# Attention followed by an ELU feed-forward layer on one core: block products in slots of seven, and q and k of batches 3 to 7 turned by DMA through DRAM

## The chip, the core and the metric

The kernel runs on one of the eight cores of a Trainium2 chip. A core has TensorE (PE in the profile; PEld is its weight load), VectorE (DVE), ScalarE (ACT), GpSimd (POOL) and SyncE (SP), each with its own instruction queue that runs in program order; they meet at semaphores. DMA transfers are issued from SP's, ACT's or POOL's queue and are carried by 16 DMA engines. The metric is the device time of one execution in microseconds; each figure below is the median of several runs.

## The reference, cut to what matters

```python
# q, k, v: [B=8, H=8, S=576, D=64]; beacon_k, beacon_v: [8, 8, 16, 64]
k_all = concat([beacon_k, k], axis=2)          # 592 keys
v_all = concat([beacon_v, v], axis=2)
scores = (q @ k_all.T) / sqrt(D)               # causal among the 576, all 16 beacons seen
a = softmax(scores)
attn = a @ v_all                               # [8, 8, 576, 64]
x = attn as [4608 tokens, 512]
h = x @ w_in                                   # w_in [512, 2048]
g = where(h > 0, h, exp(min(h, 0)) - 1)        # ELU
out = g @ w_out                                # w_out [2048, 512], out [4608, 512] fp32
```

## The kernel before

**Attention.** It works batch by batch, and within a batch by pairs of heads `p` = 0 to 3 (two heads of 64 fill 128 partitions). The scores are computed with keys on the partitions and queries along the free dimension, so q and k are both needed with D on the partitions ("turned"). `load_qk` (L117) casts q and k from fp32 to bf16 while loading them into stage tiles `qst` and `kst` (two buffers each) of 96 partitions, six consecutive rows of the sequence on each partition, in runs of 384 numbers. `T` (L225) turns a pair with 24 small PE transposes (12 of q, 12 of k) into a PSUM tile of the tag `S`; `ck` (L248) copies that tile with ACT into one of four `qk` tiles, putting the rows back in order; `cb` (L242) puts the beacon keys into the first 16 columns with DVE.

`S` (L266) computes a quarter of a pair's scores into a PSUM tile of the tag `S` (two buffers), `x` (L286) takes their exponential with ACT, `m` (L292) masks the diagonal blocks with DVE. `L` and `W` (L323, L361) multiply the exponentials with ones and with v for four heads at a time; their results lie in tiles of the tag `S` too. `n` (L342) turns the sums into reciprocals with ACT (logarithm, then exponential, tile `rl`), and `M` (L390) multiplies by them with DVE and so writes `xT`, the input of the feed-forward layer. `R` (L412) does the last 64 queries of a batch in the same way. `load_v` (L124) loads v with GpSimd, the beacon values first and then five transfers, into one of two buffers.

**Feed-forward layer.** The tokens are cut into ten tiles `t` (two of 256, eight of 512). `F` (L427) computes 128 of the 2048 columns of `h` with four matmuls of 512 columns into one of two PSUM banks `hps`; `e` (L444), `r` (L449) and `g` (L455) make the ELU of it with ACT, DVE and DVE, and `g` writes it to `gt`. From tile 2 on, the second product is a block scheme with seven products instead of eight: the sums of blocks that it needs are made by `wt` (L506, of the weights) and `Z` (L506 to L516, of `gt`) with DVE; each of the seven phases of `PH` (L519) is 16 matmuls of 256 columns, eight for each half `qd`, accumulated in two PSUM tiles. `J` (L536) takes a phase's result away: phases 0, 2 and 3 by an ACT copy to `sm`, phases 1, 4 and 5 by a DVE addition to `osb`, phase 6 by an ACT copy to `osb`; SP's queue stores each `osb` (three buffers).

**Order.** The order on every engine is the order in which the program is written. Up to the end of tile 2 it is written out by hand, as a list of words such as `S.2.0.1` (L573 to L607). From then on a loop over `b` = 3 to 10 writes it (L628): for each of 16 slots `i`, first the ELU column `F e r g` of tile `b`, then, in the 14 slots of `HS`, one half phase `Q` of tile `b-1` and, after its second half, `J`; then the sums `Z` that `SUMS` puts there; then what `todo` holds for the slot of batch `b`: scores (`SC`), `L` and `W` (`LW`, `WR`), and up to `b` = 7 the transposes `T_` of the last pair of batch `b` and of three pairs of batch `b+1`. At `i` = 3 the loads of batch `b+1` are issued on POOL, q and k (`lk`) and then v (`lv`).

Of the kernel before, what the change touches and what calls it, by code (L numbers as in the profile page):

```python
# [10 lines left out]
BF16 = mybir.dt.bfloat16  # L11
# [6 lines left out]
def kernel(  # L18
# [21 lines left out]
    R = 6  # L40
# [4 lines left out]
    NKC = (SK + P - 1) // P  # L45
# [24 lines left out]
    NFC = DF // P  # L70
# [6 lines left out]
    _sets = list(get_activation_tables(nc.m.arch).items())  # L77
    _set_id = next(i for i, (nm, fs) in enumerate(_sets) if _needed.issubset(fs))

    konst = ctx.enter_context(tc.tile_pool(name="konst", bufs=1))  # L80
    stage = ctx.enter_context(tc.tile_pool(name="stage", bufs=2))
    attn = ctx.enter_context(tc.tile_pool(name="attn", bufs=2))
    xpool = ctx.enter_context(tc.tile_pool(name="xpool", bufs=3))
# [8 lines left out]
            name=nc.get_next_instruction_name(),  # L92
# [9 lines left out]
    NPR = NFC // 2  # L102
# [9 lines left out]
    def new_stage(b):  # L112
        qst = stage.tile([PR, H, R, D], BF16, tag="qst")
        kst = stage.tile([PR, H, R, D], BF16, tag="kst")
        st.setdefault(b, [None] * 3)[0:2] = [qst, kst]

    def load_qk(b, h0, h1):  # L117
        for src, dst in ((q, st[b][0]), (k, st[b][1])):
            nc.gpsimd.dma_start(
                out=dst[:, h0:h1, :, :].rearrange("p h r d -> p h (r d)"),  # L120
                in_=src[b, h0:h1, :, :].rearrange("h (p r) d -> p h (r d)", r=R),
            )
# [39 lines left out]
    for t in qks:  # L162
# [4 lines left out]
    bkT = konst.tile([P, NP, P], BF16)  # L167
# [7 lines left out]
        out=triu, in_=triu, compare_op=ALU.is_ge, fill=0.0, base=0,  # L175
# [13 lines left out]
    op = {}  # L189
# [31 lines left out]
    tps, qkT, sc, ets = {}, {}, {}, {}  # L221
# [98 lines left out]
    lt, ut, rls = {}, {}, {}  # L320
# [185 lines left out]
    def Z(t, n, h_):  # L506
# [8 lines left out]
        else:  # L515
# [3 lines left out]
    PH = [(0, (0, 0), B11, True), (1, (1, 0), B21, True), (0, (0, 0), T2, False), (1, (0, 1), T1, True),  # L519
          (0, None, B12, False), (1, (1, 0), B22, False), (0, (1, 1), T4, False)]  # L520

    @step
    def Q(t, ph, qd):

        if (t, 0) not in xy:
            for n_ in (0, 1) if t % 2 == 0 else (1, 0):
                xy[t, n_] = psum.tile([P, 2, HM], FP32, tag="ops", name="ops")
        n_, src, wt_, first = PH[ph]
        for c in range(NPR):
            lw = s3[:, c] if src is None else A(t, c // HP, *src)[:, c % HP]  # L530
            nc.tensor.matmul(  # L531
                out=xy[t, n_][:, qd, :], lhsT=lw[:, P * qd:P * (qd + 1)], rhs=wt_[:, c, :],
                start=(first and qd == 0 and c == 0), stop=(c == NPR - 1), skip_group_check=True)
# [20 lines left out]
    def wo(i):  # L554
        load_wo(i)

    @step
    def lk(b):
        new_stage(b)
        load_qk(b, 0, H)  # L560

    @step
    def lv(b):
# [24 lines left out]
    F.1.0 r.1.1 g.1.1 S.1.3.2 e.1.0 m.1.3.0 r.1.0 x.1.3.2 S.1.2.0 x.1.2.0 F.1.2 G.0.0.1 g.1.0 e.1.2  # L588
    S.1.3.3 S.1.2.1 m.1.3.2 F.1.5 m.1.2.0 x.1.3.3 cb.2.2 x.1.2.1 r.1.2 S.1.2.2 e.1.5 g.1.2 F.1.3
    m.1.3.3 G.0.1.1 x.1.2.2 m.1.2.1 r.1.5 e.1.3 g.1.5 m.1.2.2 S.1.2.3 r.1.3 T.2.0 x.1.2.3 ck.2.0  # L590
    g.1.3 F.1.6 F.1.7 S.2.0.0 S.2.0.1 e.1.6 cb.3.0 x.2.0.0 x.2.0.1 G.0.0.2 S.2.0.2 m.1.2.3 x.2.0.2
    G.0.1.2 T.2.1 r.1.6 g.1.6 e.1.7 m.2.0.0 T.2.2 m.2.0.1 ck.2.1 m.2.0.2 G.0.0.3 ck.2.2 L.1.0 r.1.7
    W.1.0.0 g.1.7 S.2.0.3 o.0.0 n.1.0 cb.2.3 F.1.4 M.1.0.0 x.2.0.3 e.1.4 m.2.0.3 G.0.1.3 r.1.4
    W.1.0.1 o.0.1 L.1.1 M.1.0.1 g.1.4 W.1.1.0 n.1.1 W.1.1.1 M.1.1.0 R.1 S.2.1.0 M.1.1.1 x.2.1.0
    G.1.1.0 n.1.R m.2.1.0 M.1.R F.2.1 F.2.0 e.2.1 S.2.1.1 S.2.1.2 e.2.0 r.2.1 g.2.1 G.1.1.1 r.2.0
    F.2.2 x.2.1.1 S.2.2.0 x.2.1.2 S.2.2.1 g.2.0 m.2.1.1 e.2.2 F.2.3 x.2.2.0 m.2.1.2 x.2.2.1 r.2.2
    G.1.0.0 e.2.3 g.2.2 m.2.2.0 m.2.2.1 r.2.3 F.2.4 S.2.2.2 g.2.3 e.2.4 S.2.1.3 cb.3.2 x.2.2.2 r.2.4
    g.2.4 G.1.1.2 F.2.5 m.2.2.2 T.3.0 x.2.1.3 m.2.1.3 e.2.5 T.2.3 ck.3.0 ck.2.3 F.2.6 r.2.5 G.1.1.3
    g.2.5 e.2.6 S.2.2.3 S.2.3.0 F.2.8 o.1.1 cb.3.1 x.2.2.3 G.1.0.1 r.2.6 x.2.3.0 S.2.3.1 m.2.2.3
# [24 lines left out]
    SLOTS = [0, 1, 2, 4, 5, 6, 7, 8, 9, 11, 12, 13]
    HS = [0, 1, 2, 3, 4, 5, 7, 8, 9, 10, 11, 12, 14, 15]
    SUMS = {0: [(-1, 1, 1)], 2: [(-1, 2, 0)], 3: [(-1, 2, 1)], 5: [(-1, 4, 0)], 7: [(-1, 4, 1)],
            11: [(0, 3, 0)], 13: [(0, 1, 0)], 15: [(0, 3, 1)]}
    for b in range(3, NT // TT + 2):  # L628
        todo = {}
        if b < B:  # L630
            todo = dict(zip(SLOTS, [
                lambda: SC(b, 1, 0), lambda: SC(b, 1, 2), lambda: (T_(b, 3), LW(b, 0)),
                lambda: SC(b, 2, 0), lambda: SC(b, 2, 2), lambda: (T_(b + 1, 0), WR(b, 0)),
                lambda: SC(b, 3, 0), lambda: SC(b, 3, 2), lambda: (T_(b + 1, 1), LW(b, 1)),
                lambda: SC(b + 1, 0, 0), lambda: SC(b + 1, 0, 2), lambda: (T_(b + 1, 2), WR(b, 1))]))
# [18 lines left out]
_INS = ['q', 'k', 'v', 'beacon_k', 'beacon_v', 'moe_w_in', 'moe_w_out']  # L654
_OUTS = [((4608, 512), 'float32')]
# [25 lines left out]
```

## Time and profile before

| | us |
|---|---|
| median of the 3 runs shown | 377.95 |
| lowest and highest of them | 377.32 and 377.96 |
| the profiled execution, its own time | 377.59 |
| its span, from the first to the last instruction | 375.9 |

| engine | busy, us | share of the span |
|---|---|---|
| PE, matmul | 352.2 | 94% |
| DVE | 286.5 | 76% |
| ACT | 253.7 | 67% |
| PE, weight load | 219.8 | 58% |
| POOL | 68.5 | 18% |

The granted TensorE clock was 0.997 over the span. The software DMA queue (POOL's) carried 54,720 packets and 18.49 MB, SP's queue 9,856 packets and 9.57 MB. HBM read was 37.22 MB, written 9.44 MB.

How to read the rows that follow. A group of instructions: line, engine, operation, output <- input by the program's names (`sc` scores, `et` exponentials, `tp` transposed pair, `hps` columns of h, `ops` block products), shapes, xcount | busy us, mean ns of one | idle time of the engine just before them, and what ended most of it. A row of a timeline: start in us, us, engine, line, operation, and in brackets the idle time before it with what ended it. A row of windows: the stretch, its length, then busy us and instruction count of PE, PEld, DVE, ACT and POOL, the granted clock, the share of the 16 DMA engines (can exceed 1, where packets overlap) and GB/s. A row of waits: who <- for whom: us in total, times, longest.

### The profile page before, as it was taken

How to read it: one execution, taken by the hardware profiler on the slowest of the kernel's cores; microseconds unless marked ns; L12 is line 12 of the kernel's file. 1: busy time of each engine (PE TensorE's matmuls, PEld its weight loads, DVE VectorE, ACT ScalarE, POOL GpSimd, SP SyncE). 2: the span in 40 equal slices, each digit the busy share in tenths (PEclk: the TensorE clock that was granted, in tenths of full speed). 3: DMA queues.
4: the chain of work that ended last, by engine and by line, in shares of the span. 5: the costliest groups of instructions: out<-in, count | busy, mean ns of one | idle time of the engine just before them, and what ended most of it. 6: DMA issues, size and time to landing. Idle time of an engine off the chain costs nothing.

```text
span 375.9 us, 11164 instructions
## 1 busy us (share of the span) xinstructions
PE 352.2 (94%) x4811; PEld 219.8 (58%) x4811; DVE 286.5 (76%) x675; ACT 253.7 (67%) x383; POOL 68.5 (18%) x100
## 2 busy tenths in 40 slices
PE   7989999999888999899989999899989998998985
PEld 3567666454555665566655666566645665665674
DVE  2448877779788697787877787868878888888861
ACT  2999996887676867697668768686767354344321
POOL 8876630410330004100510040000000000000000
PEclk9999999999999999999999999999999999999998
DMA  8999999963298019900973057001000100110112
GB/s 117 170 186 197 179 190 196 74 103 81 17 59 149 3 58 95 151 6 30 102 101 77 14 71 70 28 2 59 31 28 2 60 28 30 47 39 29 56 58 85
DMA packets 65201, 28.89 MB, mean 77 GB/s; under 512 B 41088, under 2 KB 63616, under 8 KB 65152
## 3 DMA queue, kind: packets, MB, share of 16 engines
q0 software_dynamic: 54720, 18.49, 44.7%
q1 hardware_dynamic: 9856, 9.57, 7.7%
q8 instruction: 37, 0.61, 0.7%
q10 hardware_dynamic: 576, 0.13, 0.2%
q14 instruction: 12, 0.10, 0.1%
HBM read 37.22 MB, written 9.44 MB: 124 GB/s over the span
## 4 chain that ended last, share of the span: by engine, by line
PE 57%; DVE 20%; ACT 10%; issue 5%; POOL 3%; DMA 3%; ACTq 0%; DVEq 0%; POOLq 0%
PE hps L436 22%; PE ops L531 18%; DVE gt L459 5%; PE lt L314 5%; PE sc L277 5%; ACT et L287 4%; DVE r L451 4%; PE ops L468 3%; DVE xT L384 3%; PE tp L235 3%; DVE osb L547 3%; DVE gt L489 2%; DMA kst<-in_k_dram 2%; PE ut L314 2%; ACT rl L350 2%
## 5 line engine op out<-in xcount | busy, mean ns | idle before, releaser
L436 PE MATMUL hps<-xT,w_in 128*128 128x512 f16 (+1 forms) x640 | 147.7, 359 | 4.4 <-DVE gt L459 3.5
L446 ACT ACTIVATE e<-hps 128x512 f32<-128x512 f32 x144 | 86.5, 601 | 53.4 <-PE hps L436 52.2
L287 ACT ACTIVATE et<-sc 128x832 f16<-128x832 f32 x128 | 104.2, 873 | 21.3 <-PE sc L277 21.3
L459 DVE TENSOR_TENSOR gt<-hps,r 128x512 f16<-128x512 f32 x144 | 99.6, 691 | 6.5 <-PE sc L277 0.5
L531 PEld LDWEIGHTS <-gt 128*128 128x128 f16 x768 | 74.5, 98 | 38.0 <-DVE gt L489 11.5
L436 PEld LDWEIGHTS <-w_in 128*128 128x128 f16 x640 | 56.3, 97 | 51.7 <-issue 12.0
L451 DVE TENSOR_SCALAR r<-e 128x512 f16<-128x512 f32 x144 | 62.5, 434 | 16.2 <-ACT e L446 14.4
L531 PE MATMUL ops<-wt,gt 128*128 128x256 f16 x384 | 50.5, 273 | 9.3 <-DVE gt L489 9.3
L303 DVE TENSOR_TENSOR et<-et,triu 128x256 f16<-128x256 f16 (+2 forms) x164 | 39.8, 271 | 23.3 <-ACT et L287 21.8
L531 PE MATMUL ops<-w_out,gt 128*128 128x256 f16 x384 | 49.1, 273 | 0.0
L277 PE MATMUL sc<-qk 64*128 64x208 bf16 (+9 forms) x528 | 36.6, 249 | 2.0 <-ACT et L287 1.1
L256 ACT COPY qk<-tp 128x1152 bf16<-128x1152 bf16 x29 | 32.5, 1134 | 3.9 <-PE tp L235 3.8
L132 POOL DMA_DIRECT2D v<-in_v_dram x40 | 34.2, 885 | 4.6 <-DMA kst<-in_k_dram 2.6
L489 DVE TENSOR_TENSOR gt<-gt 128x1024 f16<-128x1024 f16 x48 | 32.5, 682 | 0.1
L277 PEld LDWEIGHTS <-qk 64*128 64x128 bf16 x528 | 19.0, 94 | 22.6 <-issue 16.0
L314 PEld LDWEIGHTS <-v 128*32 128x32 f16 x1248 | 21.2, 94 | 9.2 <-issue 2.5
L127 POOL DMA_DIRECT2D v<-in_beacon_v_dram x8 | 4.3, 534 | 115.0 <-PE ut L314 115.0
L384 DVE TENSOR_TENSOR xT<-lt,rl 128x448 f16<-128x448 f32 (+6 forms) x28 | 10.6, 419 | 15.4 <-ACT rl L350 15.4
L547 DVE TENSOR_TENSOR osb<-ops,sm 128x512 f32<-128x512 f32 x24 | 16.4, 682 | 5.6 <-issue 4.6
L540 ACT COPY sm<-ops 128x512 f32<-128x512 f32 x24 | 14.1, 586 | 8.3 <-PE ops L531 8.3
L314 PE MATMUL ut<-et,v 128*32 128x64 f16 (+6 forms) x840 | 16.9, 224 | 1.1 <-issue 0.6
L468 PE MATMUL ops<-w_out,gt 128*128 128x512 f16 x64 | 16.5, 380 | 0.0
(55 smaller groups left out, 249.2 us busy)
## 6 DMA issues: line engine op xcount, KB each, us to landing
out_dram<-osb SPq DMA_DIRECT2D x36, 256.0 KB, 2.2
qst<-in_q_dram POOLq DMA_DIRECT2D x6, 576.0 KB, 6.5
kst<-in_k_dram POOLq DMA_DIRECT2D x6, 576.0 KB, 9.4
v<-in_v_dram POOLq DMA_DIRECT2D x24, 128.0 KB, 5.1
w_in<-in_moe_w_in_dram POOLq DMA_DIRECT2D x16, 128.0 KB, 5.3
w_out<-in_moe_w_out_dram POOLq DMA_DIRECT2D x4, 512.0 KB, 11.0
v<-in_v_dram POOLq DMA_DIRECT2D x8, 112.0 KB, 3.3
v<-in_v_dram POOLq DMA_DIRECT2D x8, 80.0 KB, 5.2
```

The lines of the kernel that those rows point to most:

```text
L132: nc.gpsimd.dma_start(out=st[b][2][r0:r0 + n, j, :, :], in_=v[b, :, ilo[j]:ilo[j] + n, :].rearrange("h s d -> s h d"),)
L256: nc.scalar.copy(out=t[:, :, NB:SK].rearrange("c i (p r) -> c i p r", r=R), in_=tps[b, p][:, :, 0:S].rearrange("c i (r p) -> c i p r", r=R))
L277: nc.tensor.matmul(out=s[:, h, a - c0:e - c0], lhsT=t[D * h:D * (h + 1), 1, P * j:P * (j + 1)], rhs=t[D * h:D * (h + 1), 0, NB + qa + a - ...
L287: nc.scalar.activation(out=ets[b, p][:, :, GW * g:GW * (g + 1)], in_=sc[b, p, g][:, :, 0:GW], func=AFT.Exp, bias=0.0, scale=SCALE)
L303: nc.vector.tensor_tensor(out=o, in0=o, in1=triu[0:kc[j], :, t0:t0 + e - a], op=ALU.mult)
L314: nc.tensor.matmul(out=t[32 * i:32 * (i + 1), a - qa:e - qa], lhsT=ones[0:kc[j], :] if half is None else v16[0:kc[j], j, h, 32 * half:32 * ...
L436: nc.tensor.matmul(out=h[:, n_, :], lhsT=w_in16[:, cc, P * fc:P * (fc + 1)], rhs=xt[k][:, cc, a - TT * k:e - TT * k], start=(cc == 0), sto ...
L446: nc.scalar.activation(out=eb[t, i], in_=flat(hp[t, i]), func=AFT.Exp, bias=0.0, scale=1.0)
L451: nc.vector.tensor_scalar(out=rb[t, i], in0=eb[t, i], scalar1=1.0, scalar2=1.0, op0=ALU.min, op1=ALU.subtract)
L459: nc.vector.tensor_tensor(out=gh[k][:, i % UN, :], in0=flat(hp[t, i]), in1=rb[t, i], op=ALU.max)
L489: nc.vector.tensor_tensor(out=o_, in0=a_, in1=b_, op=op_)
L531: nc.tensor.matmul(out=xy[t, n_][:, qd, :], lhsT=lw[:, P * qd:P * (qd + 1)], rhs=wt_[:, c, :], start=(first and qd == 0 and c == 0), stop= ...
```

## The change

Three things are changed.

1. **Block products.** `Q` takes a range of the 112 matmuls of a tile (7 phases x 2 halves x 8) instead of a phase and a half. Each of the 16 slots gets `NQ` = 7 of them; `HS` goes. `J` of a phase is written behind the slot in which its last matmul lies (`i` = 2, 4, 6, 9, 11, 13 and 15). In `SUMS` two sums move one slot ahead: the second half of sum 4 from `i` = 7 to 6, the first half of sum 1 from 13 to 12.
2. **q and k from batch 3 on.** `lk` casts q and k of a batch with two GpSimd DMAs from DRAM to DRAM into a bf16 scratch laid out by row [S, H, D] (two buffers each). A new step `lt` issues four DMA transposes on SP's queue, each turning 576 rows of 256 columns (two pairs) into half of a stage tile that now holds the turned q and k of two pairs; GpSimd writes the zeros behind the keys and copies the beacon keys. `T`, `ck` and `cb` of these batches go. In the loop `lt` of batch `b+1` is written at `i` = 1, `lv` of batch `b+1` stays at `i` = 3, and `lk` of batch `b+2` comes at `i` = 4. In the list `lt.3` stands where `T.3.0` stood, and `lk.4` is added near its end.
3. **Three sums of tile 2** (`Z.2.3.0`, `Z.2.1.0`, `Z.2.3.1`) move from the head of `b` = 3 into the last lines of the list.

```diff
+    BD = 3
+    dram = ctx.enter_context(tc.tile_pool(name="dram", bufs=2, space=bass.MemoryType.DRAM))
...
-    def Q(t, ph, qd):
+    def Q(t, k0, k1):
...
-        n_, src, wt_, first = PH[ph]
-        for c in range(NPR):
+        for k_ in range(k0, k1):
+            ph, qd, c = k_ // (2 * NPR), k_ // NPR % 2, k_ % NPR
+            n_, src, wt_, first = PH[ph]
...
     def lk(b):
-        new_stage(b)
-        load_qk(b, 0, H)
+        if b < BD:
+            new_stage(b)
+            load_qk(b, 0, H)
+            return
+        for n_, src in enumerate((q, k)):
+            t = scr[b, n_] = dram.tile([S, H, D], BF16, tag=f"scr{n_}", name="scr")
+            nc.gpsimd.dma_start(out=t[:, :, :], in_=src[b].rearrange("h s d -> s h d"))
+
+    @step
+    def lt_(b):
+
+        for x_, tag in enumerate(("qst", "kst")):
+            t = stage.tile([P, 2, 2, P * NKC], BF16, tag=tag, name="qkd")
+            for n_ in range(2):
+                nc.sync.dma_start_transpose(
+                    out=t[:, :, n_, NB:SK],
+                    in_=scr[b, n_].rearrange("s h d -> s (h d)")[:, 2 * P * x_:2 * P * (x_ + 1)])
+            nc.gpsimd.memset(t[:, :, 1, SK:P * NKC], 0.0)
+            nc.gpsimd.tensor_copy(out=t[:, :, 1, 0:NB], in_=bkT[:, 2 * x_:2 * x_ + 2, NB * b:NB * (b + 1)])
+            for y in range(2):
+                qkT[b, 2 * x_ + y] = t[:, y, :, :]
...
-    HS = [0, 1, 2, 3, 4, 5, 7, 8, 9, 10, 11, 12, 14, 15]
-    SUMS = {0: [(-1, 1, 1)], 2: [(-1, 2, 0)], 3: [(-1, 2, 1)], 5: [(-1, 4, 0)], 7: [(-1, 4, 1)],
-            11: [(0, 3, 0)], 13: [(0, 1, 0)], 15: [(0, 3, 1)]}
+    NQ = 14 * NPR // NFC
+    SUMS = {0: [(-1, 1, 1)], 2: [(-1, 2, 0)], 3: [(-1, 2, 1)], 5: [(-1, 4, 0)], 6: [(-1, 4, 1)],
+            11: [(0, 3, 0)], 12: [(0, 1, 0)], 15: [(0, 3, 1)]}
...
         if b == 3:
-            run("wt.3.0 wt.3.1 Z.2.3.0 Z.2.1.0 Z.2.3.1")
+            run("wt.3.0 wt.3.1")
...
-            if i in HS:
-                n_ = HS.index(i)
-                run(f"Q.{b - 1}.{n_ // 2}.{n_ % 2}")
-                if n_ % 2:
-                    run(f"J.{b - 1}.{n_ // 2}")
+            run(f"Q.{b - 1}.{NQ * i}.{NQ * (i + 1)}")
+            for ph in range(7):
+                if NQ * i < 2 * NPR * (ph + 1) <= NQ * (i + 1):
+                    run(f"J.{b - 1}.{ph}")
...
+            if i == 1 and b + 1 < B:
+                run(f"lt.{b + 1}")
+            if i == 4 and b + 2 < B:
+                run(f"lk.{b + 2}")
             if i == 3 and b + 1 < B:
-                run(f"lk.{b + 1} lv.{b + 1}")
+                run(f"lv.{b + 1}")
```

More of the change, by code (lines that the diff above doesn't have):

```diff
@@ L555, in wo @@
         load_wo(i)
+    scr, qkd = {}, {}
     @step
     def lk(b):
-        new_stage(b)
-        load_qk(b, 0, H)
+        if b < BD:
[17 more added lines that the diff above has]
+                qkT[b, 2 * x_ + y] = t[:, y, :, :]
+    op["lt"] = lt_
     @step
@@ L590 @@
     m.1.3.3 G.0.1.1 x.1.2.2 m.1.2.1 r.1.5 e.1.3 g.1.5 m.1.2.2 S.1.2.3 r.1.3 T.2.0 x.1.2.3 ck.2.0
-    g.1.3 F.1.6 F.1.7 S.2.0.0 S.2.0.1 e.1.6 cb.3.0 x.2.0.0 x.2.0.1 G.0.0.2 S.2.0.2 m.1.2.3 x.2.0.2
+    g.1.3 F.1.6 F.1.7 S.2.0.0 S.2.0.1 e.1.6 x.2.0.0 x.2.0.1 G.0.0.2 S.2.0.2 m.1.2.3 x.2.0.2
     G.0.1.2 T.2.1 r.1.6 g.1.6 e.1.7 m.2.0.0 T.2.2 m.2.0.1 ck.2.1 m.2.0.2 G.0.0.3 ck.2.2 L.1.0 r.1.7
@@ L596 @@
     F.2.2 x.2.1.1 S.2.2.0 x.2.1.2 S.2.2.1 g.2.0 m.2.1.1 e.2.2 F.2.3 x.2.2.0 m.2.1.2 x.2.2.1 r.2.2
-    G.1.0.0 e.2.3 g.2.2 m.2.2.0 m.2.2.1 r.2.3 F.2.4 S.2.2.2 g.2.3 e.2.4 S.2.1.3 cb.3.2 x.2.2.2 r.2.4
-    g.2.4 G.1.1.2 F.2.5 m.2.2.2 T.3.0 x.2.1.3 m.2.1.3 e.2.5 T.2.3 ck.3.0 ck.2.3 F.2.6 r.2.5 G.1.1.3
-    g.2.5 e.2.6 S.2.2.3 S.2.3.0 F.2.8 o.1.1 cb.3.1 x.2.2.3 G.1.0.1 r.2.6 x.2.3.0 S.2.3.1 m.2.2.3
+    G.1.0.0 e.2.3 g.2.2 m.2.2.0 m.2.2.1 r.2.3 F.2.4 S.2.2.2 g.2.3 e.2.4 S.2.1.3 x.2.2.2 r.2.4
+    g.2.4 G.1.1.2 F.2.5 m.2.2.2 lt.3 x.2.1.3 m.2.1.3 e.2.5 T.2.3 ck.2.3 F.2.6 r.2.5 G.1.1.3
+    g.2.5 e.2.6 S.2.2.3 S.2.3.0 F.2.8 o.1.1 x.2.2.3 G.1.0.1 r.2.6 x.2.3.0 S.2.3.1 m.2.2.3
     L.2.0 e.2.8 x.2.3.1 W.2.0.0 g.2.6 W.2.0.1 m.2.3.0 s.0.0 r.2.8 g.2.8 s.0.1 m.2.3.1 F.2.7 wt.1.0 n.2.0
@@ L603 @@
     F.2.10 wt.2.1 x.2.3.3 G.1.0.3 e.2.10 S.3.0.2 m.2.3.3 o.1.0 x.3.0.2 S.3.0.3 F.2.12 wt.4.0 r.2.10 m.3.0.2 g.2.10
-    L.2.1 e.2.12 W.2.1.0 x.3.0.3 s.1.0 r.2.12 F.2.14 wt.4.1 g.2.12 m.3.0.3 n.2.1 M.2.1.0 F.2.13 e.2.14
-    T.3.1 W.2.1.1 e.2.13 r.2.14 R.2 ck.3.1 T.3.2 g.2.14 r.2.13 F.2.15 g.2.13 M.2.1.1 n.2.R M.2.R
-    e.2.15 r.2.15 ck.3.2 g.2.15
-    """)
-    def T_(b, p):
-        if b < B:
-            run(f"cb.{b}.{p} T.{b}.{p} ck.{b}.{p}")
+    L.2.1 e.2.12 W.2.1.0 x.3.0.3 s.1.0 lk.4 r.2.12 F.2.14 wt.4.1 g.2.12 Z.2.3.0 m.3.0.3 n.2.1 M.2.1.0 F.2.13 e.2.14
+    W.2.1.1 e.2.13 r.2.14 R.2 g.2.14 Z.2.1.0 r.2.13 F.2.15 g.2.13 M.2.1.1 n.2.R M.2.R
+    e.2.15 r.2.15 g.2.15 Z.2.3.1
+    """)
     def SC(b, p, g0):
@@ L631 @@
             todo = dict(zip(SLOTS, [
[L632 to L635, printed above, removed]
+                lambda: SC(b, 1, 0), lambda: SC(b, 1, 2), lambda: LW(b, 0),
+                lambda: SC(b, 2, 0), lambda: SC(b, 2, 2), lambda: WR(b, 0),
+                lambda: SC(b, 3, 0), lambda: SC(b, 3, 2), lambda: LW(b, 1),
+                lambda: SC(b + 1, 0, 0), lambda: SC(b + 1, 0, 2), lambda: WR(b, 1)]))
         if b == 3:
-            run("wt.3.0 wt.3.1 Z.2.3.0 Z.2.1.0 Z.2.3.1")
+            run("wt.3.0 wt.3.1")
         for i in range(NFC):
```

## The prediction

> **What bounds the kernel now.** I read the page first, then the waits, then one stage at a time. A stage is one round of the loop over `b`, cut at the first `F` matmul of each tile; a slot is one value of its inner index `i`.
>
> ```profile
> span 375.9 us, 11164 instructions
> PE 352.2 (94%) x4811; PEld 219.8 (58%) x4811; DVE 286.5 (76%) x675; ACT 253.7 (67%) x383; POOL 68.5 (18%) x100
> ```
>
> The table of windows (us; then busy us and instructions of PE, PEld, DVE, ACT, POOL; clock; DMA share; GB/s) has `b` = 5, 7, 8 and 10:
>
> ```profile
> core 0: us, PE busy (x) PEld busy (x) DVE busy (x) ACT busy (x) POOL busy (x), PEclk, DMA share, GB/s
> ...
> 184.01:224.37 40.36, 38.94 (x576) 24.42 (x576) 32.28 (x78) 30.42 (x47) 6.33 (x9) 1.00 0.53 72
> ...
> 264.74:302.68 37.94, 36.01 (x489) 22.24 (x489) 30.69 (x70) 24.68 (x40) 0.00 (x0) 1.00 0.09 30
> 302.68:330.38 27.70, 26.53 (x176) 17.09 (x176) 24.02 (x44) 11.53 (x20) 0.00 (x0) 1.00 0.11 38
> ...
> 358.09:375.90 17.81, 12.56 (x114) 10.79 (x111) 6.84 (x11) 2.93 (x5) 0.00 (x0) 0.94 0.22 74
> ```
>
> In a full stage PE works 38.94 of 40.36 us and everything else has room: PE's own work sets the period, and DVE, at 32.28, is the next bound. Most of the 1.42 us that PE is idle has one cause, which the waits (total, times, longest) name:
>
> ```profile
> PE ops L531 <- DVE gt L489: 9.3, 8, 1.3
> ```
>
> Eight times, once for each `b` from 3 to 10, the block products wait for a sum `Z`. The timelines of PE and of DVE show why:
>
> ```profile
> 196.87 0.61 PE L531 MATMUL ops<-wt,gt 128*128 128x256 f16 x4 [1.29 <-DVE gt L489]
> ...
> 195.53 0.68 DVE L547 TENSOR_TENSOR osb<-ops,sm 128x512 f32<-128x512 f32 x1
> 196.13 0.68 DVE L489 TENSOR_TENSOR gt<-gt 128x1024 f16<-128x1024 f16 x1
> ```
>
> At `i` = 3 `J` of phase 1 is written ahead of `Z.2.1`. It cannot run before phase 1 has ended, so `Z` ends 0.7 us later still, and the fifth product of phase 2, which reads it, stands.
>
> **Part 1: PE transposes and their copies go** (20 pairs: all of batches 3 to 7). First the groups of the stage `b` = 5, then PE's order at one pair:
>
> ```profile
> L235 PE MATMUL tp<-identb,qst 96*64 96x96 bf16 x48 | 1.8, 209 | 0.0
> L235 PE MATMUL tp<-identb,kst 96*64 96x96 bf16 x48 | 1.7, 206 | 0.0
> ...
> L245 DVE COPY qk<-bkT 128x16 bf16<-128x16 bf16 x4 | 0.7, 175 | 0.0
> ...
> L256 ACT COPY qk<-tp 128x1152 bf16<-128x1152 bf16 x4 | 4.5, 1132 | 0.7 <-PE tp L235 0.7
> ```
> ```profile
> 190.45 0.45 PE L235 MATMUL tp<-identb,qst 96*64 96x96 bf16 x12
> 190.73 0.42 PE L235 MATMUL tp<-identb,kst 96*64 96x96 bf16 x12
> 191.08 0.76 PE L314 MATMUL lt<-et,ones 128*32 128x512 f16 x20
> ```
>
> Busy times of pipelined matmuls overlap their neighbours, so I price a pair by starts: 191.08 - 190.45 = 0.63 us, 2.5 us for four, and 2.6 with the gaps around them. ACT loses 4.5 us and DVE 0.7 us a stage, which buys nothing directly. Stages `b` = 3 to 6 have four pairs, `b` = 7 has one, the hand-written list three. **Gain: 4 x 2.6 + 0.6 = 11.0 us**, and 0.5 of 1.9 in the list, because there DVE is nearly full, as the window of the list's end shows:
>
> ```profile
> 84.00:103.20 19.20, 17.23 (x308) 9.05 (x308) 16.43 (x40) 13.78 (x22) 3.08 (x4) 1.00 0.31 56
> ```
>
> **Part 2: seven products in each slot instead of eight in 14 of 16.** The 112 matmuls cost the same. What changes is order: phase 1 now ends inside `i` = 4, so `J` of phase 1 comes behind `Z.2.1`, and the product that needs that sum moves to `i` = 5, behind one more `F` (four matmuls, about 0.87 us). **Gain: the 9.3 us.** It holds for `b` = 10 too, where no `F` runs. What is late next: sum 4 moves from `i` = 7 to `i` = 6, ahead of the `M` there. A score buffer (tag `S`, two of them) is freed by that `M`:
>
> ```profile
> 203.59 0.75 DVE L384 TENSOR_TENSOR xT<-ut,rl 128x192 f16<-128x192 f32 x2
> ...
> 204.51 0.53 PE L277 MATMUL sc<-qk 64*128 64x416 bf16 x6
> ```
>
> `M` ended 0.17 us before the scores of `i` = 7. Now it ends some 0.6 us later by DVE's own work (+0.68 for `Z`, less the copy of 0.18), and the scores come earlier. With two buffers, one no longer turned by `tp`, the second score group of `i` = 7 should wait some 0.6 us. **Cost: 5 x 0.6 = 3.0 us**, between 0 and 1.3 a stage (a whole wait as before).
>
> **Part 3: three sums move from the head of stage 3 into the list.**
>
> ```profile
> 104.43 0.69 DVE L489 TENSOR_TENSOR s<-gt 128x1024 f16<-128x1024 f16 x1
> 105.15 0.69 DVE L489 TENSOR_TENSOR gt<-gt 128x1024 f16<-128x1024 f16 x1
> 105.76 0.69 DVE L489 TENSOR_TENSOR s<-gt 128x1024 f16<-128x1024 f16 x1
> ...
> 107.56 1.02 PE L436 MATMUL hps<-xT,w_in 128*128 128x512 f16 x4 [1.66 <-DVE gt L459]
> ```
>
> These 2 us lie before the `gt` for which PE waits 1.66. In the list they can fill what DVE stands idle there:
>
> ```profile
> 99.86 0.76 DVE L384 TENSOR_TENSOR xT<-ut,rl 128x384 f16<-128x384 f32 x2 [1.10 <-PE ut L314]
> 101.36 0.49 DVE L404 TENSOR_TENSOR xT<-ut,rl 128x128 f16<-128x128 f32 x2 [0.75 <-ACT rl L350]
> ```
>
> **Gain: 1.0** of 1.66, since not every idle moment has a sum ready.
>
> **Part 4: casts to DRAM and DMA transposes.** They must hide. No row shows a small write into DRAM, nor a DMA transpose. A batch's two casts are 9216 pieces (S x H rows of 64 numbers, 256 B read, 128 B written). Two views of the DMA, 40 slices each (of 0.175 and of 0.2 us), bound them:
>
> ```profile
> DMA  3094001769999988989999999999999999999300
> ...
> q0 software_dynamic: 4832, 0.61, 136.2%
> ```
> ```profile
> DMA  0009936579999999999999999999999999999998
> ...
> q0 software_dynamic: 1568, 1.18, 102.0%
> ```
>
> The first is `v`, pieces of the same shape into SBUF: 4832 packets, from slice 3 to 38, 6.3 us. The second is today's `q` and `k`: 1568 packets of 768 B, from slice 4 to 40, 7.4 us. So a batch's casts take between 9216/4832 x 6.3 = 12 us and 9216/1568 x 7.4 = 43 us. I take 14, nearest to `v`, whose pieces they are. The Trainium skill ("DMA: Bandwidth & Descriptors", Specifications) speaks against it: below 512 B a transfer becomes a read-modify-write; if that doubles a piece, the estimate is 28 us. No row here shows it: `v` is below 512 B too, but goes to SBUF.
>
> The transposes move 4 x 288 KB a batch, 1.18 MB, as much as the loads of the second view write. Below: half of their 7.4 us, as those read 4 bytes for 2 written, 3.7 us; above: 4608 rows of 256 B at the price of the 768 B packets, 22 us. I take 8, by that view's bytes. The same page ("Latency and other measured facts") gives 261 GB/s for transposes, by which it would be 4.5 us.
>
> Is there cover? Time: `lk` of a batch is issued right behind `lv` of the batch before, when POOL gets its `v` buffer, nearly a stage and a half ahead of the first score. Throughput: 6.3 + 14 + 8 = 28 us of a 37 us stage. Queues: POOL's extra memsets and copies stand before a `v` load that waits anyway. The four transposes stand on SP ahead of output stores, and behind them could wait only `J`'s buffers (three): stores land in 2.2 us, and SP spends most of its time waiting.
>
> ```profile
> POOL v L127 <- PE ut L314: 115.0, 5, 28.4
> ...
> SPq L550 <- DVE osb L547: 137.9, 18, 22.4
> ```
> ```profile
> out_dram<-osb SPq DMA_DIRECT2D x36, 256.0 KB, 2.2
> ```
>
> The tight place is batch 3: POOL reaches its load at 53.55, `v` of batch 2 is in front of it, and its first score is in the second row here:
>
> ```profile
> 53.55 0.78 POOL L119 DMA_DIRECT2D qst<-in_q_dram  x1 [1.75 <-PE sc L277]
> ...
> 85.53 0.84 PE L277 MATMUL sc<-qk 64*128 64x416 bf16 x6
> ```
>
> With `v`'s 6.3 us in front the casts run from about 58; to 85 there are 27 us, enough for casts of 14 and the first transposes; casts over 20 us would stall PE there. **Cost: 0.**
>
> **The sum.** 11.0 + 0.5 + 9.3 + 1.0 - 3.0 = 18.8 us. Taken from the profiled execution's 377.59 (span 375.9 and 1.7 around it): 358.8. That execution is 0.36 under the median of 377.95, within the scatter of the runs shown. I say **358.8**; the stage `b` = 5 should last 40.36 - 2.6 - 1.3 + 0.6 = 37.1, and `b` = 8 about 26.7.
>
> **The rivals.**
> - *DVE becomes the bound.* A stage leaves it 32.28 - 0.70 = 31.6 us of work, plus waits for ACT's `rl`, 3.4 us in the groups of `b` = 5:
>
> ```profile
> L303 DVE TENSOR_TENSOR et<-et,triu 128x256 f16<-128x256 f16 (+2 forms) x20 | 5.0, 275 | 2.9 <-ACT et L287 2.6
> ...
> L384 DVE TENSOR_TENSOR xT<-lt,rl 128x192 f16<-128x192 f32 (+1 forms) x4 | 1.5, 420 | 2.7 <-ACT rl L350 2.7
> ...
> L404 DVE TENSOR_TENSOR xT<-ut,rl 128x128 f16<-128x128 f32 x2 | 0.5, 286 | 0.7 <-ACT rl L350 0.7
> ```
>
> That is 35.0, below 37.1, but close. If the waits for `et` (2.6 below) stay whole as well it is 37.6. Were it 38.6 a stage, five stages give back 1.5 each: **366**. If the `Z` wait only moves to another phase, the 9.3 us stay and it is 368. Against: `b` = 8 runs DVE at 24.02 of 27.70 without other waits. 0.13.
> - *Batch 3's scratch is late.* Casts of 20 to 27 us stall PE once at its first score, 0 to 12 us, also by DVE behind SP's blocked stores: **362 to 371**. 0.13.
> - *Casts set the pace: slower than before.* With casts of L us a batch, the DMA must carry five of them, four loads of `v` and five sets of transposes from 58 us on, before the first score of batch 7. In my forecast that comes at 241 us: stage 5 begins at 184.01 less 1.5 and less 3.3 for each of two stages, 175.9; one more stage of 37.1; and 28 us to `i` = 11. 58 + 5L + 4 x 6.3 + 5 x 8 = 241 gives L = 23.6. From L = 27.4 (241 + 19 us) the gain is eaten; at 43 us the score comes at 338, and the time is **456**. Against: the pieces of `v`, of the same size, run at L = 12. 0.13. By the page's rule on small transfers, L doubled to 28, the kernel would be about as slow as now or slower.
> - *No net change*, losses meeting the gain by chance: 0.04.
>
> **How the numbers follow.** The forecast (355 to 362) has 0.57. The range takes it, the first rival and most of the second, **354.5 to 369**; its lower end is without the 3.0 us and with all of the list's gain. The third rival lies outside. This kernel's time can be told from no change beyond about 0.2%, 0.75 us. Faster: 0.57 + 0.13 + 0.13 = 0.83; same 0.04; slower 0.13.
>
> **What would show it.** Right: PE 480 matmuls fewer, no `tp`; the wait of L531 for L489 gone; stage `b` = 5 near 37.1 with PE over 97% busy; scores waiting for `M` at `i` = 7; software queue near 93,000 packets (54,720 + 5 x 7,680), written bytes up by 5.9 MB. Wrong: scores waiting for DMA, or SP blocked for a stage (casts or transposes dear); the wait for `gt` on L436 growing (DVE the bound). I am most wrong if a small piece written to DRAM costs more than about 1.8 times one written to SBUF.

## The result, and the profile after

| | us |
|---|---|
| before, median of 4 runs | 377.69 (377.32 to 377.96) |
| after, median of 4 runs | 366.47 (366.07 to 368.11) |
| ratio after / before, with its 95% interval | 0.971 (0.968 to 0.974) |
| predicted | 358.8, range 354.5 to 369.0 |

The kernel became faster, by 11.2 us instead of 18.8. One run of those below, of the version with a third cast, was in a slower state (378.96 us) and is not counted. The page of the kernel after has these lines, in the order of those shown of before: the span, the engines, the costliest line of PE, and VectorE's `r`.

```profile
span 364.4 us, 10239 instructions
PE 343.1 (94%) x4331; PEld 210.1 (58%) x4331; DVE 290.8 (80%) x655; ACT 232.9 (64%) x363; POOL 87.0 (24%) x120
...
L438 PE MATMUL hps<-xT,w_in 128*128 128x512 f16 (+1 forms) x640 | 148.4, 360 | 11.2 <-DVE gt L461 10.8
...
L453 DVE TENSOR_SCALAR r<-e 128x512 f16<-128x512 f32 x144 | 72.3, 502 | 15.0 <-ACT e L448 13.3
```

PE has the 480 matmuls fewer that were predicted. But two rows are odd. DVE has 20 instructions fewer and is busy 4.3 us longer (290.8 against 286.5). And `r`, which no edit touched, takes 502 ns in the mean; in the page of before it took 434:

```profile
L451 DVE TENSOR_SCALAR r<-e 128x512 f16<-128x512 f32 x144 | 62.5, 434 | 16.2 <-ACT e L446 14.4
```

The view of PE's waits (total, times, longest) has no wait of the block products for `Z` any more. The wait for `gt` has grown instead; the first row is of before, the second of after:

```profile
PE hps L436 <- DVE gt L459: 3.5, 6, 1.7
...
PE hps L438 <- DVE gt L461: 10.8, 12, 3.8
```

`gt` is computed from `r`. VectorE's timeline has four long `r`s, of 4.22, 3.60 and twice 2.10 us (the one at 151.18 is not shown), beside ordinary ones of 0.43 (start, duration):

```profile
70.87 4.22 DVE L453 TENSOR_SCALAR r<-e 128x512 f16<-128x512 f32 x1 [0.49 <-ACT e L448]
...
107.00 0.68 DVE L491 TENSOR_TENSOR s<-gt 128x1024 f16<-128x1024 f16 x1
107.59 1.29 DVE L491 TENSOR_TENSOR w_out<-w_out 128x1024 f16<-128x1024 f16 x2
108.80 3.60 DVE L453 TENSOR_SCALAR r<-e 128x512 f16<-128x512 f32 x1
...
186.29 0.43 DVE L453 TENSOR_SCALAR r<-e 128x512 f16<-128x512 f32 x1
...
188.85 2.10 DVE L453 TENSOR_SCALAR r<-e 128x512 f16<-128x512 f32 x1 [0.20 <-ACT e L448]
```

GpSimd's timeline at the same times:

```profile
70.40 2.23 POOL L570 DMA_DIRECT2D scr<-in_q_dram  x1
72.09 2.75 POOL L570 DMA_DIRECT2D scr<-in_k_dram  x1
...
107.66 2.26 POOL L570 DMA_DIRECT2D scr<-in_q_dram  x1
109.36 2.78 POOL L570 DMA_DIRECT2D scr<-in_k_dram  x1
...
186.07 2.42 POOL L570 DMA_DIRECT2D scr<-in_q_dram  x1
188.03 2.67 POOL L570 DMA_DIRECT2D scr<-in_k_dram  x1
```

GpSimd is issuing the two casts of a batch, back to back, 2.2 to 2.8 us each. The held `r`s end at 75.09, 112.40 and 190.95; the issue of the second cast ends at 74.84, 112.14 and 190.70. So each ends 0.25 to 0.26 us after that issue, whether it began early in the pair or late. The two sums of `w_out` at 107.59, which have two inputs, run in the first 1.2 us of the issue at 107.66 and take 1.29 together, no longer per sum than `s` just before it (0.68). Nor is every operation with one input held. At batch 3's second cast, issued from 56.48 to 58.67, VectorE copies `osb` out of PSUM at 57.38 in its usual 0.69 us, while the small bf16 copy of the beacon keys that starts at 57.99 takes 0.68 us instead of some 0.18.

The Trainium skill ("SBUF — State Buffer", Who interferes with whom) has a rule of this form: VectorE in its two-port mode, which copies, casts and tensor-scalar operations can enter, and GpSimd share a port pair that the one locks against the other for a whole instruction, and the writing of DMA descriptors by GpSimd needs it. The trace agrees for `r` against `w_out`, with 4.22 and 3.60 us against some 0.65 each; the page tells mostly of the other direction, VectorE starving a DMA of descriptors.

PE, which waited for `gt`, then also runs slower for a while. Its timeline has the two waits, and the windows behind them the granted clock (after the five engines' busy times):

```profile
75.87 1.02 PE L438 MATMUL hps<-xT,w_in 128*128 128x512 f16 x4 [3.37 <-DVE gt L461]
...
113.17 1.02 PE L438 MATMUL hps<-xT,w_in 128*128 128x512 f16 x4 [3.78 <-DVE gt L461]
```
```profile
75.80:81.00 5.20, 5.13 (x34) 2.12 (x35) 3.19 (x10) 2.26 (x4) 0.00 (x0) 0.67 1.96 200
112.00:119.00 7.00, 5.83 (x59) 3.13 (x59) 5.27 (x13) 2.22 (x5) 0.64 (x3) 0.76 2.39 153
119.00:125.00 6.00, 6.00 (x51) 3.61 (x50) 5.74 (x13) 4.59 (x8) 0.00 (x0) 1.00 0.14 44
```

After 3.37 and 3.78 us of idleness the clock is lower in the mean. Windows of one microsecond of the same trace have 0.50 from 77 to 80 and from 115 to 117, less than 1.00 in the one beside each end, and 1.00 from 81 and from 118 on: each time the clock is halved for some 3.4 us, and the rows above are means over that and the full clock. So a wait costs more than its length, by at most 1.7 us each time (an estimate: half of 3.4).

### The profile page after: what moved, and what is told of

It reads as the page before. It is cut to its first block, busy times and chain, and to the rows that moved or that the text cites. A ratio compares the mean times of both kernels' runs of the same rounds, so it can differ in the third digit from the quotient of the medians.

```text
span 364.4 us, 10239 instructions
## 1 busy us (share of the span) xinstructions
PE 343.1 (94%) x4331; PEld 210.1 (58%) x4331; DVE 290.8 (80%) x655; ACT 232.9 (64%) x363; POOL 87.0 (24%) x120
## 4 chain that ended last, share of the span: by engine, by line
PE 63%; DVE 21%; ACT 4%; issue 4%; POOL 4%; DMA 3%; ACTq 0%; DVEq 0%; POOLq 0%
PE hps L438 27%; PE ops L534 20%; DVE r L453 7%; PE sc L279 5%; PE lt L316 5%; DVE gt L461 5%; PE ops L470 3%; DVE xT L386 2%; PE ut L316 2%; DMA kst<-in_k_dram 2%; DVE osb L550 2%; ACT e L448 2%; DVE et L305 1%; DVE s L491 1%; POOL v L134 1%
## 5 line engine op out<-in xcount | busy, mean ns | idle before, releaser
L438 PE MATMUL hps<-xT,w_in 128*128 128x512 f16 (+1 forms) x640 | 148.4, 360 | 11.2 <-DVE gt L461 10.8
L453 DVE TENSOR_SCALAR r<-e 128x512 f16<-128x512 f32 x144 | 72.3, 502 | 15.0 <-ACT e L448 13.3
L534 PE MATMUL ops<-wt,gt 128*128 128x256 f16 x384 | 52.5, 273 | 0.0
L534 PE MATMUL ops<-w_out,gt 128*128 128x256 f16 x384 | 51.8, 274 | 0.0
L305 DVE TENSOR_TENSOR et<-et,triu 128x256 f16<-128x256 f16 (+2 forms) x164 | 38.7, 269 | 14.9 <-ACT et L289 14.3
L134 POOL DMA_DIRECT2D v<-in_v_dram x40 | 34.2, 869 | 3.4 <-DMA kst<-in_k_dram 2.7
L279 PE MATMUL sc<-qkd 64*128 64x208 bf16 (+5 forms) x320 | 22.3, 252 | 0.3
L386 DVE TENSOR_TENSOR xT<-lt,rl 128x448 f16<-128x448 f32 (+6 forms) x28 | 10.6, 419 | 12.2 <-ACT rl L352 12.2
L581 POOL MEMSET qkd<- 128x96 bf16 x10 | 6.0, 641 | 55.0 <-issue 48.6
L316 PE MATMUL ut<-et,v 128*32 128x64 f16 (+6 forms) x840 | 17.2, 225 | 1.3 <-issue 1.0
L279 PEld LDWEIGHTS <-qkd 64*128 64x128 bf16 x320 | 11.2, 94 | 11.9 <-issue 9.3
L349 ACT ACTIVATE rl<-lt 128x512 f32<-128x512 f32 (+1 forms) x15 | 9.1, 604 | 13.3 <-PE lt L316 13.3
## 6 DMA issues: line engine op xcount, KB each, us to landing
scr<-in_q_dram POOLq DMA_DIRECT2D x5, 576.0 KB, 13.8
scr<-in_k_dram POOLq DMA_DIRECT2D x5, 576.0 KB, 17.2
```

The lines of the kernel that those rows point to most:

```text
L134: nc.gpsimd.dma_start(out=st[b][2][r0:r0 + n, j, :, :], in_=v[b, :, ilo[j]:ilo[j] + n, :].rearrange("h s d -> s h d"),)
L279: nc.tensor.matmul(out=s[:, h, a - c0:e - c0], lhsT=t[D * h:D * (h + 1), 1, P * j:P * (j + 1)], rhs=t[D * h:D * (h + 1), 0, NB + qa + a - ...
L305: nc.vector.tensor_tensor(out=o, in0=o, in1=triu[0:kc[j], :, t0:t0 + e - a], op=ALU.mult)
L316: nc.tensor.matmul(out=t[32 * i:32 * (i + 1), a - qa:e - qa], lhsT=ones[0:kc[j], :] if half is None else v16[0:kc[j], j, h, 32 * half:32 * ...
L438: nc.tensor.matmul(out=h[:, n_, :], lhsT=w_in16[:, cc, P * fc:P * (fc + 1)], rhs=xt[k][:, cc, a - TT * k:e - TT * k], start=(cc == 0), sto ...
L453: nc.vector.tensor_scalar(out=rb[t, i], in0=eb[t, i], scalar1=1.0, scalar2=1.0, op0=ALU.min, op1=ALU.subtract)
```

## The experiments

Three theories were set against each other. **P**: the 7.6 us missing from the forecast go to the issue of the casts, which holds up a one-input `r`; it hangs on how long GpSimd issues without a break. **D**: the traffic of the casts and transposes on the DMA engines slows the kernel. **V**, the prediction's first rival: VectorE's own work and order have become the bound. The first four runs shared one chip and its runs of before (377.45), the next four another (378.18), the last two a third (377.41).

**The even spread and the moved sums alone**, on the kernel before, with its loads and PE transposes:

```diff
-    HS = [0, 1, 2, 3, 4, 5, 7, 8, 9, 10, 11, 12, 14, 15]
+    NQ = 14 * NPR // NFC
...
-            run("wt.3.0 wt.3.1 Z.2.3.0 Z.2.1.0 Z.2.3.1")
+            run("wt.3.0 wt.3.1")
```

> The even spread and the moved sums alone, on the kernel before: q and k are still turned on PE. All theories: the waits of the block products for Z go (9.3 us), so 367.5 to 369.5 us, with no r (TENSOR_SCALAR f16<-f32) over 0.8 us, since no cast to DRAM is issued. Above 371 the sums or the score buffers would give back part of it.

Measured: 363.88 us, ratio 0.964 (0.962 to 0.965), below the expected range and below the kernel after. So this part gains 13.6 us by itself, more than the whole change. Its PE waits:

```profile
PE hps L436 <- DVE gt L459: 2.8, 9, 0.5
```

No row has the block products waiting for a sum, and no wait for `gt` is over 0.5 us.

**The DMA path alone**: casts and transposes as in the kernel after, with the old slots and sums.

```diff
-    NQ = 14 * NPR // NFC
-    SUMS = {0: [(-1, 1, 1)], 2: [(-1, 2, 0)], 3: [(-1, 2, 1)], 5: [(-1, 4, 0)], 6: [(-1, 4, 1)],
-            11: [(0, 3, 0)], 12: [(0, 1, 0)], 15: [(0, 3, 1)]}
+    HS = [0, 1, 2, 3, 4, 5, 7, 8, 9, 10, 11, 12, 14, 15]
+    SUMS = {0: [(-1, 1, 1)], 2: [(-1, 2, 0)], 3: [(-1, 2, 1)], 5: [(-1, 4, 0)], 7: [(-1, 4, 1)],
+            11: [(0, 3, 0)], 13: [(0, 1, 0)], 15: [(0, 3, 1)]}
```

> The casts and DMA transposes alone, with the old slots of the block products. If the parts add up: the changed kernel plus the 9.3 us of Z waits less the score waits, 373 to 376 us, and again four r of 2 to 4 us while GpSimd issues casts. Under 370 would say that the stalls of r and the Z waits hide each other.

Measured: 382.22 us, ratio 1.012 (1.011 to 1.014): slower than before by 1.2%, though PE has 480 matmuls fewer to do. The expectation missed it. PE's waits name both costs:

```profile
PE hps L438 <- DVE gt L461: 15.4, 13, 3.7
PE ops L534 <- DVE gt L491: 9.2, 8, 1.3
```

The wait for `Z` is the old one, 9.2 against 9.3, so it is the new slots and sums that take it away, and not the DMA path. The wait for `gt` is 15.4: the long `r`s last 4.22, 3.60, 3.62 and 3.61 us here, and a fifth 1.77, where two of the four of after last only 2.10.

**`r` with two inputs** where casts are issued: the 32 `r` of tiles 0 and 1 and of the first four columns of tiles 2 to 5 take a tile of ones in place of the second constant.

```diff
-        nc.vector.tensor_scalar(
-            out=rb[t, i], in0=eb[t, i], scalar1=1.0, scalar2=1.0, op0=ALU.min, op1=ALU.subtract)
+        if t in (0, 1) or (t in (2, 3, 4, 5) and i < 4):
+            nc.vector.scalar_tensor_tensor(
+                out=rb[t, i], in0=eb[t, i], scalar=1.0, in1=ones512, op0=ALU.min, op1=ALU.subtract)
```

> As the changed kernel, but r of tiles 0 and 1 and of the first four columns of tiles 2 to 5 reads a second tensor (a tile of ones) in place of a constant, about 0.2 us longer each. Theory P (r and GpSimd's descriptor writing exclude each other): no r over 1 us, the PE waits of 3.4 and 3.8 us and the slow clock behind them go, 355 to 359 us. Theory D (traffic of casts and transposes on the DMA engines slows the kernel): unchanged, 365 to 368. Theory V (DVE is full): slower than the changed kernel, 367 to 370.

Measured: 357.53 us, ratio 0.947 (0.946 to 0.949). The groups of VectorE in this run:

```profile
L459 DVE TENSOR_SCALAR r<-e 128x512 f16<-128x512 f32 x112 | 48.0, 429 | 7.2 <-ACT e L450 6.0
...
L456 DVE SCALAR_TENSOR_TENSOR r<-e,ones 128x512 f16<-128x512 f32 x32 | 22.0, 689 | 4.0 <-ACT e L450 3.1
```

Each changed `r` costs 0.26 us more (689 against 429 ns), 8.3 us of VectorE's time in all, and the kernel is 8.9 us faster. V, by which more work for VectorE must cost, falls; so does D, as the traffic is the same. The casts are issued as before, at 72.21 and 73.90:

```profile
72.21 2.25 POOL L576 DMA_DIRECT2D scr<-in_q_dram  x1
73.90 2.77 POOL L576 DMA_DIRECT2D scr<-in_k_dram  x1
```

and an `r` in the midst of them goes through in its usual time:

```profile
73.11 0.69 DVE L456 SCALAR_TENSOR_TENSOR r<-e,ones 128x512 f16<-128x512 f32 x1
...
75.11 0.69 DVE L456 SCALAR_TENSOR_TENSOR r<-e,ones 128x512 f16<-128x512 f32 x1 [0.20 <-ACT e L450]
```

**Each cast in four DMAs** of 144 rows, the same bytes and pieces:

```diff
-            nc.gpsimd.dma_start(out=t[:, :, :], in_=src[b].rearrange("h s d -> s h d"))
+            for s0 in range(0, S, 144):
+                nc.gpsimd.dma_start(out=t[s0:s0 + 144, :, :], in_=src[b, :, s0:s0 + 144, :].rearrange("h s d -> s h d"))
```

> As the changed kernel, but each cast is issued as four of 144 rows. Theory P: each issue holds r up for at most its own descriptors; if GpSimd lets go between issues no r exceeds 1.3 us and the time is 358 to 362 us, if not r stays at 2 to 4 us and the time at 366. Theory D: the traffic is the same, 365 to 368.

Measured: 355.84 us, ratio 0.943 (0.941 to 0.945), the lowest median of all versions, though two below are within 0.7 us of it: 10.6 us under the kernel after, below the expected range, with `r` as it was. D, with the same traffic, would have 365 to 368. PE's wait for `gt`, 10.8 us in after, is now

```profile
PE hps L438 <- DVE gt L461: 5.0, 11, 1.2
```

GpSimd issues longer in all, 3.69 and 4.21 us for one pair of casts:

```profile
103.58 3.69 POOL L571 DMA_DIRECT2D scr<-in_q_dram  x4
106.88 4.21 POOL L571 DMA_DIRECT2D scr<-in_k_dram  x4
```

but an `r` that starts in it is held for the rest of one short issue only; the first one here ends at 105.69, 0.25 us after the second of the four issues (104.38 to 105.44):

```profile
104.70 0.99 DVE L453 TENSOR_SCALAR r<-e 128x512 f16<-128x512 f32 x1
...
107.32 0.56 DVE L453 TENSOR_SCALAR r<-e 128x512 f16<-128x512 f32 x1
```

**A third cast in each batch.** It copies q once more into a scratch tile that nobody reads; that part is extra work.

```diff
+        t = dram.tile([S, H, D], BF16, tag="extra", name="extra")
+        nc.gpsimd.dma_start(out=t[:, :, :], in_=q[b].rearrange("h s d -> s h d"))
```

> As the changed kernel, with a third cast for each batch (q once more, into a scratch that nobody reads). Theory P: the issue of each batch lasts some 2 us longer, so the four long r grow to about 6, 5.5, 4 and 4 us and the time to 372 to 377 us. Theory D (traffic): 7 us more of a DMA that has room for it, up to 1 us. A rival to P, that r waits for something else which happens at the same time (the transposes, which are issued near by): unchanged, 365 to 368.

Measured: ratio 0.985 (0.979 to 0.992), single runs from 369.75 to 375.21 us: some 6 us slower than the kernel after, in runs that scatter over 5.5 us. VectorE's and GpSimd's timelines, at the place that was shown of after:

```profile
106.66 5.82 DVE L453 TENSOR_SCALAR r<-e 128x512 f16<-128x512 f32 x1
```
```profile
105.52 2.26 POOL L570 DMA_DIRECT2D scr<-in_q_dram  x1
107.21 2.79 POOL L570 DMA_DIRECT2D scr<-in_k_dram  x1
109.18 3.04 POOL L572 DMA_DIRECT2D extra<-in_q_dram  x1
```

The issue now ends at 112.22 and the `r` at 112.48, 0.26 later: the hold grows with the issue, through three DMAs in a row. The two later batches have an `r` of 4.31 and of 4.32 us. At batch 4 the three issues stand apart, and each holds an `r` of its own, for 2.00, 2.05 and 1.86 us, again to 0.25 or 0.26 us after its end. VectorE's own work is that of the kernel after, so V would expect no change; D expects at most 1 us.

**Eight DMAs of 72 rows** for each cast (`range(0, S, 72)` in the edit of the four):

> As the changed kernel, each cast issued as eight of 72 rows. Theory P with the port free between issues: as with four pieces or slightly better, 354.5 to 356.5 us, longest r under 1 us.

Measured: 356.51 us, ratio 0.943 (0.941 to 0.945), as with four. Shorter pieces of issue bring nothing more; the longest `r` is 0.87 us.

**Casts at another place**, whole as in the kernel after: `lk` of batch `b+2` is written right behind `lt` at `i` = 1, ahead of the `v` load, and `lk.4` in the list likewise.

```diff
-            if i == 4 and b + 2 < B:
-                run(f"lk.{b + 2}")
+                if b + 2 < B:
+                    run(f"lk.{b + 2}")
```

> As the changed kernel with whole casts, but on GpSimd's queue the casts of a batch stand ahead of the v loads, so that they are issued near the middle of a stage and not in its first slots. Theory P: r is still held up by 2 to 4 us for each batch, but DVE is less loaded there: 361 to 366 us. If the place does not matter: 366.

Measured: 360.39 us, ratio 0.954 (0.951 to 0.958), just under the expected range. The longest `r` is still held for 3.52 us, but PE waits less for it:

```profile
PE hps L438 <- DVE gt L461: 7.9, 14, 1.5
```

So the price of a hold depends on the slot it falls into; that was argued beforehand and not taken apart further.

**Both, four DMAs and the new place:**

> Both: casts in four pieces and ahead of the v loads. Theory P: 354 to 356.5 us; the first stage of the loop (39.4 us with split casts, where the next lasts 36.6) gets 1 to 2 us shorter if it was the casts that lengthened it.

Measured: 356.47 us (355.58 to 360.26), ratio 0.946 (0.941 to 0.951). No gain over four DMAs alone: the two do not add up, which fits that both avoid the same wait. The first stage of the loop lasts 38.6 us instead of 39.4, a gain of 0.8 where 1 to 2 were expected.

**The even spread without the moved sums** (the edit of the first run, less the changed line `run("wt.3.0 ...")` and the lines of the list):

> The even spread on the kernel before, with the three sums of tile 2 left at the head of stage 3. If the moved sums are worth the 1.0 us of the prediction: 365 us (363.9 with them). If they carry most of what the spread gained beyond the 9.3 us of Z waits: 367 to 368.

Measured: 365.22 us, ratio 0.967 (0.966 to 0.969). Against the run with the moved sums, 1.3 us are theirs.

**Only `Z.2.1` ahead of `J`**, on the kernel before, to see whether that order is the whole of the wait that the spread removes:

```diff
-    SUMS = {0: [(-1, 1, 1)], 2: [(-1, 2, 0)], 3: [(-1, 2, 1)], 5: [(-1, 4, 0)], 7: [(-1, 4, 1)],
+    SUMS = {0: [(-1, 1, 1)], 2: [(-1, 2, 0)], 5: [(-1, 4, 0)], 7: [(-1, 4, 1)],
...
+            if i == 3:
+                run(f"Z.{b - 1}.2.1")
```

> The kernel before, with one change of order: at i = 3 the sum Z.2.1 is written ahead of the block products and of J of phase 1. If J ahead of Z makes the Z waits, as the prediction has it: they go and the time falls by 8 to 9.5 us, to 368 to 369.5. What the even spread gains beyond that (it ran at 363.9 with the moved sums) then belongs to the two empty slots and the moved sums. If the wait has another cause: 376 to 378.

Measured: 371.79 us, ratio 0.985 (0.983 to 0.986), less of a gain than expected. Among PE's waits the one for `Z` is still there:

```profile
PE ops L531 <- DVE gt L489: 4.1, 7, 0.7
```

`J` explains 5.2 of the 9.3 us. The rest is gone in the even spread, where the product that reads the sum also stands one `F` later; no run moves that product alone.

## Why the prediction was right and wrong

Stage lengths in us, worked out from the starts of the first `F` of each tile in PE's timelines (stage "2" is the list's end, tile 2):

| stage | before | spread and sums | after | four DMAs |
|---|---|---|---|---|
| 2 | 34.6 | 34.2 | 38.0 | 32.8 |
| 3 | 42.4 | 39.2 | 43.0 | 39.4 |
| 4 | 40.4 | 38.9 | 37.7 | 36.6 |
| 5 | 40.4 | 38.9 | 38.9 | 37.6 |
| 6 | 40.4 | 38.5 | 36.5 | 36.5 |
| 7 | 37.9 | 36.2 | 35.6 | 35.6 |
| 8 | 27.7 | 26.4 | 26.4 | 26.4 |

**Part 4, "Cost: 0", is the step that failed.** The prediction looked for cover in the DMA engines' time, in SP's queue and in GpSimd's place ahead of a `v` load "that waits anyway". It asked what GpSimd's longer issue delays on GpSimd, and not whom it delays elsewhere. The runs put the cost at 366.47 - 355.84 = 10.6 us. By the profiled executions, which differ by 10.0, it is 5.2 in stage 2, 3.6 in stage 3, 1.1 and 1.3 in stages 4 and 5, less 1.0 by which the version with four DMAs enters stage 2 later. Of it, 5.8 is PE's wait for `gt` (10.8 less 5.0), and at most 3.4 the halved clock behind the two longest waits (the estimate above, twice). Stages 6 and 7, in which no cast is issued, are alike with and without the division.

The sum with all its terms, each step a run:

| term | predicted | measured | from |
|---|---|---|---|
| even spread, with the wait for `M` | 9.3 - 3.0 = 6.3 | 12.2 | 377.41 - 365.22 |
| three sums moved | 1.0 | 1.3 | 365.22 - 363.88 |
| PE transposes out, casts in four DMAs | 11.0 + 0.5 = 11.5 | 8.0 | 363.88 - 355.84 |
| issue of the casts in one DMA each | 0 | -10.6 | 355.84 - 366.47 |

The measured terms sum to 10.9; the whole change, against its own runs of before, is 11.2. That the time came out inside the range is in good part luck: the range reached to 369 for another cause, VectorE as the bound, and the even spread brought 5.9 us more than predicted, which pays for over half of what the issue costs.

- **Part 2 was right in its mechanism and sized too small.** The wait for `Z` went, all 9.3 us; stage 8, predicted at 26.7, lasts 26.37. The 3.0 us set against it were not there: the six score matmuls of `i` = 7 take 0.76 where the prediction's row of before has 0.53, 0.2 instead of 0.6, and no wait of these matmuls for `M` is named.

```profile
203.25 0.76 PE L279 MATMUL sc<-qkd 64*128 64x416 bf16 x6
```

  The remaining 2.9 us (12.2 less 9.3) were not taken apart.
- **Part 1 was right where nothing else is late.** From the second column to the last, stages 4, 6 and 7 become shorter by 2.3, 2.0 and 0.6, against 2.6, 2.6 and 0.6. Stage 3 gains nothing: PE works 1.8 us less there (36.93 against 38.70), but waits 2.7 us for `gt` instead of 0.5. Stage 5, forecast at 37.1, lasts 38.9, and with four DMAs 37.6, a gain of 1.3. In stage 5 PE's timeline has a gap that the trace gives no releaser for, in after and with four DMAs alike (209.93, 1.17 us); its cause stays open:

```profile
219.70 0.19 PE L316 MATMUL ut<-et,v 80*32 80x64 f16 x1 [1.04 <-issue]
```

  The list (stage 2) gains 1.4 instead of 0.5.
- **Part 3** was right: 1.3 against 1.0.
- **What Part 4 had right.** The page's DMA part of the kernel after: queues (packets, MB, share), then issues (KB each, median us to landing):

```profile
q0 software_dynamic: 93120, 18.49, 60.6%
...
HBM read 37.22 MB, written 15.34 MB: 144 GB/s over the span
...
scr<-in_q_dram POOLq DMA_DIRECT2D x5, 576.0 KB, 13.8
...
scr<-in_k_dram POOLq DMA_DIRECT2D x5, 576.0 KB, 17.2
```

  Packets and bytes are as predicted. The casts landed 13.8 and 17.2 us after their issue, and the second is issued 2 us behind the first, so a batch's pair takes some 19 us at the median, above the 14 taken and below the 23.6 at which the scores would wait. No score waited for a DMA. The 28 us that the prediction had for a pair if the rule on transfers below 512 B (the Trainium skill, "DMA: Bandwidth & Descriptors", Specifications) doubles a piece are not borne out by these 19 us; whether a small write costs something extra is not separated from the transfers beside it. The transposes' issue and landing, over all 20:

```profile
L578 SPq DMA_TRANSPOSE qkd<-scr x20: 1292/2404/4078, 63.5 to 231.7; - x20
...
DMA to landing us min/median/max: 3.8/7.1/10.5
```

  A single one lands in 7.1 us at the median, and SP's queue is held 2.4 us by each, 6.0 to 12.8 us by the four of a batch, so the 8 taken for four together was low; PE's waits show nothing of it.
- **The rivals.** The first one's 366 is the measured time, and by its sign in the waits ("the wait for `gt` growing") it seems borne out; but more work for VectorE made the kernel faster. A wait for `gt` says that VectorE is late, not why. Late scratch and casts that set the pace are refuted by the scores, which never wait for a DMA.

## What to carry to other kernels

Price a DMA that GpSimd issues three times: in the DMA engines, in GpSimd's queue, and on VectorE, where a one-input operation like `r` may stand still while it is issued. Many small pieces make that time long (0.73 to 1.07 us for a `v` transfer of 640 to 1024 pieces, 2.2 to 2.8 for a cast of 4608), and dividing the DMA into several gives it back without moving a byte otherwise. When the mean duration of an instruction that nobody edited rises, look for its single long cases and at what every other engine does at their end.

## What the runs showed of the hardware

- The issue of one cast (4608 pieces) took GpSimd 2.2 to 2.8 us, and an `r` (one input, fp32 to fp16, SBUF to SBUF) held by it ended 0.25 us after the issue, or after the last of two or three in a row: up to 5.82 us instead of 0.43. Operations with two inputs were not held (a sum 0.65, the changed `r` 0.69), nor was a one-input copy out of PSUM (0.69 in the midst of an issue).
- Between issues that follow directly on one another `r` did not get in when they were whole casts (one hold lasts through the pair), but it did when the cast was divided into four (0.99 at the place of 3.60); both kinds of issue overlap in their records, and why the one lets `r` in is open. Two `r`s that began 0.22 us into an issue (186.29, above, and 148.62) were not held; why is open too.
- After PE had stood for 3.37 and 3.78 us its granted clock was 0.50 for some 3.4 us. In the run with a third cast two waits of 2.76 us were followed by 0.50 as well, and in the run with casts at another place waits of 1.55 us were not. The Trainium skill ("TensorE: Matmul & The Clock Gate", Part 1: The HAM clock gate) gives a window of about 3.4 us of idleness after which the clock is halved; the trace agrees in the half (0.50), but waits of 2.76 us, shorter than that window, were enough here.
